# First slot's steps and the fixed rows' read three half steps sooner, clearing writes with the first steps, weights' loads one place sooner

## The chip, the cores and the metric

One NeuronCore of a Trainium2 chip runs the whole kernel as one launch. The metric is the device time of that launch in microseconds (us), lower is better. Engines are called PE (TensorE, matmuls), PEld (its weight loads), DVE (VectorE), ACT (ScalarE), POOL (GpSimd) and SP (SyncE, which here issues most of the transfers). XS, SD and ZD are scratch buffers in device memory.

## The reference, cut to what matters

```python
# x: 8 x 2496 x 256, filt: 1249 x 256, 8 experts, w1: 8 x 256 x 1024, w2: 8 x 1024 x 256
X = np.fft.rfft(x, axis=1)
y = np.fft.irfft(X * (filt_r + 1j * filt_i), n=2496, axis=1)   # a long filter along the sequence
x = y.reshape(19968, 256)
xn, en = x / norm(x), expert_emb / norm(expert_emb)
logits = xn @ en.T / tau
expert_idx = argmax(logits)                      # one expert a row
gate_w = softmax(logits)[expert_idx]
for e in range(8):
    mask = expert_idx == e
    h = np.maximum(x[mask] @ w1[e], 0.0)
    out[mask] = gate_w[mask, None] * (h @ w2[e])
```

## The kernel before

**Groups and stages.** The eight batches are eight groups, 0 to 7. The transform of length 2496 is taken as 64 times 39, and every group goes through three stages. `conv_s1` (11 tiles): a tile of x is read (`in`), multiplied by a matrix of cosines (`s1_g_t` in PSUM), copied by ACT to `s` and written to the buffer SD. `conv_s2` (10 tiles): `a` is read from SD, the other half of the transform is taken (`s2_g_k`), the product with the filter `f` (read from in_filt) is formed as `yy` and `xs`, transformed back (`sa`), copied to `z` and written to ZD. `conv_sb`: `f` is read from ZD, the last matmul gives `y`, the rows of the result; these become `rows` (16-bit high and low pieces), are transposed (`tp`, `yT`) for the logits `lp`, and `route` finds each row's expert: `l`, `mx`, `oh`, `ex` on DVE and ACT, the ranks `rk` on PE, then the target addresses `ixi`. POOL scatters `rows` by these into XS, which is sorted by expert.

**Slots.** Rows sorted in XS are worked off in slots. The rows of the first six tiles of group 0 (chunk 0, twelve scatters) go to slots 0 to 7, one an expert, of 128 rows: the "fixed" slots, in areas of XS that are set to zero ahead by `clear_fixed(e)`, one write `XS<-zf` an expert. `read_pair(p)` reads the areas of two experts, each with a transposing read (`xTf`) and one of two columns (`metaf`). Later slots have 256 rows. A slot has four half steps: each does `up` (matmuls `ph`, 12 for a fixed slot, and their halves `h` by ACT and DVE) and, two steps later, `down` (matmuls `po`). The output rows are scattered by POOL.

**Weights.** Expert e's two matrices come as loads of 1024 KB (`W<-in_w`, the last expert's in pieces of 256 KB). They are prepared in steps, named by a letter, the expert and a piece in the tables below: g is a sum of squares on PE (`gram`), d, p and q make a scale of it, k makes a high 16-bit piece on ACT (`W<-W,wsc`, L324), l the low one on DVE (L331). A slot's `ph` and `po` read these pieces.

**Order.** All engines but POOL have an order written out by hand over the head of the kernel, a loop in which step n takes one step of the convolution, then what the tables give it, then a half step of a slot:

```python
for n in range(HEAD):
    next(whole_head, None)
    weights(n)          # clear_fixed at CLEAR..CLEAR+7, read_pair(0) at FIRST_ROWS, WLOADS, WPREP
    keep_warm(n)
    if n >= SLOTS:
        next(steps)
```

Steps 0 to 10 are group 0's `conv_s1`, 11 to 34 its `conv_s2`, from 35 on its `conv_sb`, with group 1's `conv_s1` between from 43. The convolution has 79 steps, so that steps 79 to 81 hold the tables' work and slots alone. After the head, half steps of slots and the convolutions of groups 1 to 7 are emitted in turn by a pace, the steps in `WLATE` with them (by the count of half steps done; slot e's first is number 4e), and a scheduler sets the order of the engines. A transfer issued by SP or ACT takes one of eight completion counters in turn; the issue waits until the transfer that had the counter eight places ahead has landed. POOL's transfers have eight of their own.

Of the kernel before, what the change touches and what calls it, by code (L numbers as in the profile page):

```python
# [46 lines left out]
DLAG = 2  # L47
MID = 8
XNEXT = 43
WLOADS = (38, 40, 42, 44, 46, 48, 50, 52, 54, 56, 58, 60, 61, 63, 78, 79)  # L50
WPREP = {43: "g00", 44: "g01", 46: "d0", 48: "p0", 49: "q0 g10", 50: "k00", 51: "l00 k01 g11", 52: "d1 l01 k02",
# [5 lines left out]
WLATE = {16: "l52 k53 p6", 17: "l53 q6 g70", 18: "k60 g71", 19: "d7 l60 k61", 20: "l61 k62", 21: "l62 k63 p7",  # L57
         22: "l63 q7", 23: "k70", 24: "l70 k71", 25: "l71 k72", 26: "l72 k73", 27: "l73"}
SIDE = 18
CLEAR, FIRST_ROWS = 39, 64  # L60
SLOTS, HEAD = 66, 82
WARM = {-1: 8, 12: 26, 35: 22, 40: 6}
FRONT = 0
FIXED = 128
# [10 lines left out]
def moe_spectral_kernel(  # L75
# [810 lines left out]
    def read_pair(p):  # L886

        xT = mp2.tile([P, 4, 256], F16, tag="xT", name=f"xTf{p}")
        for j in range(2):
            e = 2 * p + j  # L890
            meta = mpm.tile([P, 2, 2], F32, tag="meta", name=f"metaf{e}")[:, :1]
            pairs[e] = xT[:, :, j * FIXED:(j + 1) * FIXED], meta
            at = slice(e * CAP, e * CAP + FIXED)
            read_rows(0, *pairs[e], XS16[at, 0:2 * D], XS[at, D:D + 2], fixed=True)
        last.setdefault("read", last["sp"])
# [151 lines left out]
    def weights(n):  # L1047
# [3 lines left out]
        if n == FIRST_ROWS:  # L1051
            read_pair(0)
        if n in WLOADS:
            next(loads)
# [62 lines left out]

    begun, late = [], dict(WLATE)

# [132 lines left out]
```

## Time and profile before

| | |
|---|---|
| time, median of 3 runs | 1350.24 us (1348.65 to 1364.11) |
| profiled execution | 1344.95 us |
| its span | 1343.2 us |
| PE busy | 1246.3 us, 93% of the span |
| DVE, ACT, POOL busy | 938.8 (70%), 762.2 (57%), 489.2 us (36%) |
| chain of work that ended last | PE 71%, DMA 18%, DVE 4%, issue 3%, ACT 2% |
| mean granted clock of PE | 0.97 |

The profiled execution is one run beside the three. PE is the busiest engine, and most of the chain that ended last lies on it. The share of the span says little of a stretch: the kernel's first 300 us are bound now by transfers, now by short steps on several engines.

### The profile page before, as it was taken

To read this page: it belongs to the slowest core of one execution; us is meant where nothing else is said; L and a number is where in the kernel's file an instruction comes from. 1 tells how busy PE (TensorE), PEld (TensorE's weight loads), DVE (VectorE), ACT (ScalarE), POOL (GpSimd) and SP (SyncE) were. 2 spreads that over 40 slices of the span, in tenths; PEclk is the share of its full clock that TensorE was granted. 3 is DMA by queue.
4 is the path that set the end of the run, shared out by engine and by line. 5 is a ranking of instruction groups with operands and counts; after the bars stand their busy time and mean duration, and the time that the engine had idled before them with its cause. 6 is when DMAs were issued, how large, how long until landed. Compare 5 with 4: busy or idle time off the path is not lost.

```text
span 1343.2 us, 36499 instructions
## 1 busy us (share of the span) xinstructions
PE 1246.3 (93%) x11027; PEld 981.2 (73%) x11027; DVE 938.8 (70%) x3078; ACT 762.2 (57%) x1760; POOL 489.2 (36%) x569
## 2 busy tenths in 40 slices
PE   7867899959897999998999999999999999999997
PEld 2344686627584778786888788878887888889886
DVE  1455796756586688976889697868786885444664
ACT  2175466825664586667757785678465843233333
POOL 0003322264255325541464346423633175111221
PEclk9997899979998999998999999999999999999999
DMA  7899868887868697868769887777675544221221
GB/s 230 271 325 369 246 185 217 186 229 226 200 169 238 190 202 174 226 192 184 168 182 245 193 195 203 224 186 194 173 196 140 119 119 106 54 49 41 57 45 37
DMA packets 272354, 241.27 MB, mean 180 GB/s; under 512 B 167123, under 2 KB 212182, under 8 KB 270373
## 3 DMA queue, kind: packets, MB, share of 16 engines
q1 hardware_dynamic: 243965, 177.87, 52.0%
q0 software_dynamic: 24320, 57.97, 14.8%
q10 hardware_dynamic: 3880, 3.03, 0.7%
q8 instruction: 104, 1.70, 0.6%
q14 instruction: 85, 0.70, 0.2%
HBM read 122.32 MB, written 85.57 MB: 155 GB/s over the span
## 4 chain that ended last, share of the span: by engine, by line
PE 71%; DMA 18%; DVE 4%; issue 3%; ACT 2%; POOL 1%; SPq 1%; ACTq 0%; DVEq 0%; POOLq 0%
PE ph L967 27%; PE po L992 26%; PE s L444 5%; DMA yT<-rows 4%; DMA f<-ZD 3%; PE sa L444 3%; PE y L444 2%; DMA f<-in_filt 2%; DMA W<-in_w 2%; PE s L439 2%; PE sa L555 2%; DMA XS<-rows,ixi 1%; DMA SD<-s 1%; PE y L439 1%; PE lp L610 1%
## 5 line engine op out<-in xcount | busy, mean ns | idle before, releaser
L992 PE MATMUL po<-W,h 128*128 (+1 forms) x3824 | 494.4, 273 | 0.2 <-ACT h L975 0.2
L967 PE MATMUL ph<-xT,wp 128*128 128x256 f16 (+2 forms) x4224 | 471.6, 258 | 10.9 <-DMA xT<-XS 3.7
L967 PEld LDWEIGHTS <-wp 128*128 128x128 f16 x4224 | 357.7, 98 | 87.8 <-issue 41.6
L992 PEld LDWEIGHTS <-h 128*128 128x128 f16 x3824 | 361.2, 98 | 68.9 <-issue 26.4
L975 ACT ACTIVATE h<-ph 128x512 f16<-128x512 f32 (+2 forms) x384 | 201.7, 527 | 244.9 <-PE ph L967 182.2
L1007 POOL DMA_INDIRECT out_dram<-o,meta x153 | 158.5, 1036 | 305.9 <-ACT o L1006 228.6
L976 DVE SCALAR_TENSOR_TENSOR h<-ph,h 128x512 f16<-128x512 f32 (+2 forms) x384 | 227.1, 591 | 48.3 <-ACT h L975 46.6
L951 DVE COPY wp<-W 128x1024 f16 x352 | 164.8, 469 | 117.8 <-PE ph L967 115.3
L790 POOL DMA_INDIRECT XS<-rows,ixi x176 | 180.1, 1023 | 142.0 <-issue 93.8
L536 POOL TENSOR_TENSOR yy<-yy,xs 128x512 f32<-128x512 f32 x60 | 80.5, 1343 | 105.6 <-DVE xs L499 85.0
L497 DVE TENSOR_TENSOR yy<-s,f 128x256 f32<-128x256 f32 x160 | 61.3, 417 | 62.5 <-ACT xs L529 27.8
L400 POOL DMA_DIRECT2D in<-in_x x66 | 38.8, 588 | 168.8 <-DVE xp L413 57.3
L635 DVE SCALAR_TENSOR_TENSOR rows<-y,rr,rows 128x256 f16<-128x256 f32 x176 | 76.7, 477 | 23.8 <-ACT rows L632 23.1
L668 ACT ACTIVATE rows<-y 128x256 f16<-128x256 f32 x176 | 67.3, 398 | 26.5 <-PE y L439 24.3
L1006 ACT ACTIVATE o<-po,meta 128x256 f32<-128x256 f32 x148 | 64.0, 478 | 28.8 <-PE po L992 27.3
L632 ACT ACTIVATE rows<-y,rr 128x256 f16<-128x256 f32 x176 | 75.5, 496 | 7.5 <-DVE rr L673 5.8
L558 ACT COPY z<-sa 128x512 f32<-128x512 f32 x80 | 46.7, 584 | 49.9 <-PE sa L555 41.2
L465 ACT COPY s<-s 128x512 f32<-128x512 f32 x88 | 52.7, 600 | 27.8 <-PE s L439 15.9
L595 ACT COPY yT<-tp 128x512 f16<-128x512 f16 x99 | 58.6, 605 | 9.1 <-PE tp L593 5.4
L444 PE MATMUL s<-xp,c1h 117*128 117x512 f32 (+1 forms) x144 | 62.0, 438 | 0.0
L412 ACT CAST yp<-yy 128x512 fp32r<-128x512 f32 x50 | 30.9, 619 | 53.0 <-POOL yy L536 52.5
L610 PEld LDWEIGHTS <-yT 128*128 128x128 f16 x704 | 33.2, 98 | 35.5 <-DMA yT<-rows 17.9
(208 smaller groups left out, 1688.8 us busy)
## 6 DMA issues: line engine op xcount, KB each, us to landing
f<-in_filt SPq DMA_DIRECT2D x160, 256.0 KB
a<-SD SPq DMA_DIRECT2D x80, 256.0 KB
ZD<-z SPq DMA_DIRECT2D x80, 256.0 KB
f<-ZD SPq DMA_DIRECT2D x80, 240.0 KB
SD<-s SPq DMA_DIRECT2D x70, 240.0 KB
in<-in_x POOLq DMA_DIRECT2D x66, 234.0 KB
W<-in_w SPq DMA_DIRECT2D x14, 1024.0 KB
in<-in_x SPq DMA_DIRECT2D x22, 234.0 KB
```

Of the source, the lines that this page charges most:

```text
L444: nc.tensor.matmul(out_, w[:k], b, start=(n == 0), stop=(n == 2))
L536: nc.gpsimd.tensor_tensor(out=yy, in0=yy, in1=xs, op=ALU.add)
L632: nc.scalar.activation(rows[:, i, 0:D], y[:, i], AF.Copy, scale=rr[:, u:u + 1])
L635: nc.vector.scalar_tensor_tensor(out=rows[:, i, D:2 * D], in0=y[:, i], scalar=rr[:, u:u + 1], in1=rows[:, i, 0:D], op0=ALU.mult, op1=ALU.s ...
L668: nc.scalar.activation(rows[:, i, D:2 * D], y[:, i], AF.Square, accum_out=ssq[:, u + i:u + i + 1])
L790: i = nc.gpsimd.indirect_dma_start(out=XS, out_offset=bass.IndirectOffsetOnAxis(ap=ix, axis=0), in_=src, in_offset=None)
L951: last["dve"] = nc.vector.tensor_copy(wp, src)
L967: last["pe"] = nc.tensor.matmul(ph[:, fi, :size], wp[:, k * 2 + wh, fi * P:(fi + 1) * P], xT[:, xh * 2 + k, :size], start=(c == 0), stop=( ...
L975: last["act"] = nc.scalar.activation(h[:, 0, :, :size], ph[:, :, :size], AF.Relu)
L976: last["lo"] = nc.vector.scalar_tensor_tensor(out=h[:, 1, :, :size], in0=ph[:, :, :size], scalar=0.0, in1=h[:, 0, :, :size], op0=ALU.max, ...
L992: nc.tensor.matmul(self.po[:, s], h, self.Wp[:, off + wh * 1024:off + wh * 1024 + D], start=(fp == 0 and fi == 0 and c == 0), stop=(fp == ...
L1007: i = nc.gpsimd.indirect_dma_start(out=out, out_offset=bass.IndirectOffsetOnAxis(ap=self.meta[:n, s, 0:1].bitcast(I32), axis=0), in_=o, in ...
```

## The change

Only the tables and constants of the head change. The eight clearing writes go from steps 39 to 46 to steps 1 to 8. Each load of weights takes the place in which the one before it stood; the first goes from step 38 to 32. `read_pair(0)`, at step 64 before, stands at 61; the first half step of a slot at 63, not 66; the head ends with its last step of convolution. The preparation of weights up to piece l20 stays at its steps; from there on the steps move sooner by one or two in n, while they come later as counted by half steps of slots: expert 5's l50 and l51, at steps 80 and 81 (14 and 15 half steps done), come at 16 and 17.

```diff
-WLOADS = (38, 40, 42, 44, 46, 48, 50, 52, 54, 56, 58, 60, 61, 63, 78, 79)
+WLOADS = (32, 38, 40, 42, 44, 46, 48, 50, 52, 54, 56, 58, 60, 62, 75, 76)
...
-         75: "d5 l40 k41", 76: "l41 k42", 77: "l42 k43 p5", 78: "l43 q5 g60", 79: "k50 g61", 80: "d6 l50 k51",
-         81: "l51 k52"}
-WLATE = {16: "l52 k53 p6", 17: "l53 q6 g70", 18: "k60 g71", 19: "d7 l60 k61", 20: "l61 k62", 21: "l62 k63 p7",
-         22: "l63 q7", 23: "k70", 24: "l70 k71", 25: "l71 k72", 26: "l72 k73", 27: "l73"}
...
+         74: "d5 l40 k41", 75: "l41 k42", 76: "l42 k43 p5", 77: "l43 q5 g60", 78: "k50 g61"}
+WLATE = {16: "d6 l50 k51", 17: "l51 k52", 18: "l52 k53 p6", 19: "l53 q6 g70", 20: "k60 g71", 21: "d7 l60 k61",
+         22: "l61 k62", 23: "l62 k63 p7", 24: "l63 q7 k70", 25: "l70 k71", 26: "l71 k72", 27: "l72 k73", 28: "l73"}
 SIDE = 18
-CLEAR, FIRST_ROWS = 39, 64
-SLOTS, HEAD = 66, 82
+CLEAR, FIRST_ROWS = 1, 61
+SLOTS, HEAD = 63, 79
```

Lines of the changed kernel have numbers lower by one. On SP in the first stage (in0_t is tile t of x, SD0 the buffer written for group 0, zf the zeros), before:

```order
L400 DMA in0_4_258<-in_x 117x512
L467 DMA SD0_208<-s0_1_262 120x2x256
L400 DMA in0_5_265<-in_x 117x512
L467 DMA SD0_208<-s0_2_269 120x2x256
L400 DMA in0_6_272<-in_x 117x512
L467 DMA SD0_208<-s0_3_276 120x2x256
```

and now:

```order
L399 DMA in0_4_258<-in_x 117x512
L466 DMA SD0_208<-s0_1_262 120x2x256
L346 DMA XS_224<-zf_225 128x258
L399 DMA in0_5_266<-in_x 117x512
L466 DMA SD0_208<-s0_2_270 120x2x256
L346 DMA XS_224<-zf_225 128x258
L399 DMA in0_6_274<-in_x 117x512
L466 DMA SD0_208<-s0_3_278 120x2x256
```

A clear stands behind each of SD0_1 to SD0_8; they stood among the reads of f from ZD before, at f0_4 to f0_8. W0, the first load of weights, stands ahead of the write of ZD0_9, the last tile of `conv_s2(0)`; ahead of f0_7's read four loads stand behind ZD0_9 in both, ahead of f0_10's seven.

On SP at the fixed rows' read (which waits for the twelfth scatter of chunk 0 in both; in1_10 is group 1's last tile of x), before:

```order
L400 DMA in1_10_1286<-in_x 117x512
L264 DMA W_201<-in_w1 128x2048
L264 DMA W_201<-in_w2 128x2048
L878 DMA_TRANSPOSE xTf0_1393<-XS_224 128x4x128
L879 DMA metaf0_1394<-XS_224 128x2
L878 DMA_TRANSPOSE xTf0_1393<-XS_224 128x4x128
L879 DMA metaf1_1397<-XS_224 128x2
L878 DMA_TRANSPOSE xTf1_1477<-XS_224 128x4x128
L879 DMA metaf2_1478<-XS_224 128x2
```

and now:

```order
L263 DMA W_201<-in_w1 128x2048
L399 DMA in1_10_1287<-in_x 117x512
L877 DMA_TRANSPOSE xTf0_1308<-XS_224 128x4x128
L878 DMA metaf0_1309<-XS_224 128x2
L877 DMA_TRANSPOSE xTf0_1308<-XS_224 128x4x128
L878 DMA metaf1_1312<-XS_224 128x2
L263 DMA W_201<-in_w2 128x2048
L877 DMA_TRANSPOSE xTf1_1429<-XS_224 128x4x128
L878 DMA metaf2_1430<-XS_224 128x2
```

The two loads that stood ahead of pair 0, W12 and W13, now stand ahead of in1_10 and between pair 0 and pair 1.

On ACT at the end of the head (s1_9 and s1_10 are the last tiles of group 1's first stage, ex and ixi belong to the routing of tile 6, h0_0_0 is the first half of slot 0), before:

```order
L467 DMA SD1_209<-s1_9_1364 120x2x256
L465 COPY s1_10_1378<-s1_1_10_1375 128x512
L467 DMA SD1_209<-s1_10_1378 120x256
L467 DMA SD1_209<-s1_10_1378 40x256
L745 ACTIVATE ex0_6_1387<-l0_6_1367 128x80
L770 CAST ixi0_6_1432<-ix0_6_1430 128x10
L324 ACTIVATE W_201<-W_201,wsc_205 128x1024
L975 ACTIVATE h0_0_0_1455<-ph0_0_0_1442 128x2x128
```

and now:

```order
L466 DMA SD1_209<-s1_9_1372 120x2x256
L974 ACTIVATE h0_0_0_1395<-ph0_0_0_1382 128x2x128
L464 COPY s1_10_1401<-s1_1_10_1398 128x512
L466 DMA SD1_209<-s1_10_1401 120x256
L466 DMA SD1_209<-s1_10_1401 40x256
L323 ACTIVATE W_201<-W_201,wsc_205 128x1024
L974 ACTIVATE h0_0_1_1440<-ph0_0_1_1420 128x2x128
L744 ACTIVATE ex0_6_1410<-l0_6_1375 128x80
```

h0_0_0 stands ahead of the copy and the writes of s1_10, and a piece of W and h0_0_1 ahead of ex0_6. SD1_10's two writes take the counters of xTf1's second read and of metaf3, where they took those of its first and of metaf2. On PE, ph0_0_0 (12 matmuls) stands ahead of s1_1_10 and ph0_0_1 ahead of rk0_6; both stood behind rk0_6. From group 1's `conv_s2` (s2_1_0) to its first routing (rk1_0) PE has 452 matmuls ph, 222 po and 112 gram, where it had 492, 243 and 96; the other matmuls there are the same. From group 2's `conv_s2` (s2_2_0 and ph2_0_0) to the end the order is the same on every engine.

## Rows read from the trace of the kernel before

**Rows 1.** Busy time by stage: stretch, its length, engines' busy time (instructions), PEclk, DMA, GB/s

```profile
10.00:25.00 15.00, 11.43 (x28) 3.81 (x27) 3.26 (x20) 5.61 (x11) 0.00 (x0) 0.89 0.86 272
...
59.00:67.00 8.00, 6.59 (x27) 2.83 (x26) 0.22 (x1) 0.59 (x1) 0.00 (x0) 1.00 0.47 135
67.00:104.00 37.00, 26.21 (x237) 15.66 (x236) 20.63 (x70) 26.59 (x73) 2.21 (x2) 0.95 1.04 326
104.00:126.00 22.00, 15.48 (x81) 7.97 (x80) 11.04 (x51) 13.29 (x29) 13.08 (x14) 0.70 1.01 363
126.00:142.00 16.00, 8.76 (x72) 5.84 (x71) 8.93 (x25) 5.87 (x9) 0.00 (x0) 0.82 1.06 320
142.00:260.00 118.00, 113.32 (x1112) 85.39 (x1111) 95.26 (x305) 75.52 (x172) 30.31 (x42) 0.97 0.77 208
260.00:299.00 39.00, 23.92 (x177) 14.09 (x175) 24.12 (x138) 17.07 (x42) 27.45 (x28) 0.78 0.82 226
299.00:1343.00 1044.00, 1002.56 (x9212) 830.70 (x9211) 757.83 (x2421) 609.63 (x1411) 414.61 (x466) 0.99 0.64 159
```

**Rows 2.** The chain of waits, 0 to 170 us: start, length, what

```profile
19.45 3.11 DMA in<-in_x
...
90.56 13.14 DMA f<-ZD
...
125.71 10.87 DMA SD<-s
```

**Rows 3.** Timeline of PE, 60 to 165 us: start, length, instruction, [idle before <- releaser]

```profile
90.63 1.10 PE L439 MATMUL y<-f,csb_sb 120*128 120x512 f32 x2 [3.02 <-DMA f<-ZD]
...
95.85 2.04 PE L439 MATMUL y<-f,csb_sb 120*128 120x512 f32 x2 [1.56 <-DMA f<-ZD]
...
141.03 0.23 PE L753 MATMUL rk<-oh,lt 128*128 128x80 f16 x1 [5.43 <-DVE oh L743]
...
148.66 1.93 PE L439 MATMUL s<-a,c_sb 128*128 128x512 f32 x4
```

**Rows 4.** The chain of waits, 255 to 305 us

```profile
279.94 5.10 DMA XS<-rows,ixi
...
290.24 5.52 DMA XS<-rows,ixi
...
295.77 3.44 DMA xT<-XS
```

**Rows 5.** Timeline of POOL, 225 to 300 us

```profile
260.52 1.04 POOL L790 DMA_INDIRECT XS<-rows,ixi  x1 [5.07 <-issue]
```

**Rows 6.** DMA issues of the whole kernel: count, KB each

```profile
W<-in_w SPq DMA_DIRECT2D x14, 1024.0 KB
...
XS<-zf SPq DMA_DIRECT2D x8, 129.0 KB
```

**Rows 7.** Timeline of POOL, 60 to 165 us

```profile
123.15 0.98 POOL L790 DMA_INDIRECT XS<-rows,ixi  x1 [0.30 <-issue]
```

**Rows 8.** Timeline of SP, 56 to 160 us

```profile
125.44 0.89 SPq L264 DMA_DIRECT2D W<-in_w  x2
130.53 1.34 SPq L878 DMA_TRANSPOSE xTf<-XS  x1
...
138.98 0.58 SPq L879 DMA_DIRECT2D metaf<-XS  x1
...
144.28 6.66 SPq L479 DMA_DIRECT2D a<-SD  x6
```

**Rows 9.** Timeline of ACT, 60 to 165 us

```profile
104.16 0.28 ACT L745 ACTIVATE ex<-l 128x96 f32<-128x96 f32 x1 [1.10 <-DMA f<-ZD]
...
139.65 0.73 ACTq L467 DMA_DIRECT2D SD<-s  x2
```

**Rows 10.** The chain of waits, 158 to 170 us

```profile
161.29 0.67 PE ph L967 x12
161.96 0.66 PE po L992 x6
162.62 0.92 PE gram L286 x16
```

**Rows 11.** Timeline of DVE, 60 to 165 us

```profile
145.67 1.28 DVE L331 SCALAR_TENSOR_TENSOR W<-W,wsc 128x1024 f16<-128x1024 f32 x1
```

4 rows, old and new, of the table WPREP are left out of this document.

## The prediction

> **What bounds the kernel now.** I read the busy time by stage first [rows 1]. From 299 µs to the end PE is busy 1002.56 of 1044 µs, and the order of all engines there is the same in both kernels; the reader is to see that nothing of this change can act behind 299 µs but a common shift. All of it is decided in the 299 µs ahead. There the stages have different limits. In the first (10 to 25 µs) the core's DMA engines are taken 0.86 of the time at 272 GB/s and PE waits for transfers; the chain of waits [rows 2] shows an x tile's read on it (19.45, 3.11 µs). From 67 to 104 the DMA share is 1.04 at 326 GB/s, and the chain runs through a 13.14 µs read of f from ZD: this stage is bound by transfers, 14 loads of 1024 KB of weights among them [rows 6]. From 104 to 142 it is a chain of short steps on all engines, with PE at 15.48 of 22 and 8.76 of 16 µs. From 142 to 260 PE is busy 113.32 of 118, so there PE's queue, that is the work ordered ahead, sets the time. From 260 to 299 PE has 23.92 of 39: it waits for group 1's rows. The chain [rows 4] shows it: scatter after scatter on POOL to 290.24, 5.52 for the last to land, 3.44 for xT, then ph2_0_0 at 299.26. The first of them starts at 260.52 [rows 5]; 22 scatters and two output writes follow each other without a hole, so what moves the first scatter moves all that follows by as much. I work out by how much.
>
> **The change, part by part.**
> Clears in the first stage. Eight writes of 129 KB [rows 6], 1.06 MB, go onto SP's queue behind SD0_1 to SD0_8. At the stage's 272 GB/s they take 3.9 µs. Of its 15 µs, 0.14 is not taken, 2.1 µs [rows 1]. So the cost is 3.9 − 2.1 = 1.8 if every gap is filled, 3.9 if none is. I take +2.5, nearer to the first, since SP issues the clears behind the loads of the next tile and the reads run ahead. SP's own time for them is covered, as it waits for the step's copy anyway.
>
> Weights one place sooner. W0 now stands ahead of ZD0_9's write and of the first reads of ZD. 1.05 MB is 3.2 µs at 326 GB/s, and from 59 to 67 the DMA share is 0.47, which leaves 4.2 of 8 µs free. It hides unless it sits in front of that write: 0 to +1, I take +0.5. Each later load takes the place of the one before it; ahead of f0_7 there are still four behind ZD0_9, ahead of f0_10 seven, so I cost the rest at nothing; what hides it is that the stage's bytes stay the same.
>
> Clears gone from 67 to 104. 1.06 MB less at 326 GB/s is 3.2 µs. The stage's last consumer shows that bytes decide: y0_7 and y0_8 waited 3.02 and 1.56 for f from ZD [rows 3], and the landing of that read released ex0_0 at 104.16 [rows 9]. So −3.2, with 0 at the other end, if the weights fill the room; bytes that are no longer there can't cost.
>
> The fixed rows' read. It waits for the last of chunk 0's twelve scatters. That scatter started at 123.15 [rows 7]; SP sent two W loads at 125.44 (over at 126.33) and then stood until 130.53 [rows 8]: 7.4 µs from scatter to read. At the end of group 1 the same kind took 5.10 and 5.52 [rows 4]. Now one of the two W loads stands ahead of in1_10 and the other behind pair 0. I take the nearest row, 5.10: −2.3. Ends: 0, and −4.2, where the read goes out as soon as SP was free (126.33).
>
> The end of the head. Pair 1 stands behind W13, and SD1_10's two writes, issued on ACT, take completion counters that pair 1's transfers hold. Before, they went out at 139.65, right behind the last of pair 1's commands at 138.98 [rows 8, 9]. If W13 goes wholly ahead of pair 1 the wait is its 3.2 µs. Queued behind it on ACT are a piece of W, h0_0_1 and ex0_6, and a1_0's read waits for these writes. Pair 1's read would otherwise go out 2.3 sooner, which covers most of it: 0 to +3.2, I take +0.5.
>
> Slot steps sooner. ph0_0_0 now stands ahead of rk0_6, and PE idled 5.43 µs ahead of rk0_6 [rows 3], so it is covered as far as the read comes in time. That is work which PE no longer has between group 1's second stage, which begins at 148.66 there [rows 3], and that group's first routing: by the two orders 40 matmuls ph and 21 po fewer, 16 gram more. In the dense part 12 ph take 0.67, 6 po 0.66 and 16 gram 0.92 [rows 10]: 40 × 0.056 = 2.2, 21 × 0.11 = 2.3, less 0.9, that is −3.6. As PE is busy 96% of 142 to 260, it should reach the first scatter in full; the other end is 0.
>
> Sum: 2.5 + 0.5 − 3.2 − 2.3 + 0.5 − 3.6 = −5.6. It is made against the profiled execution (1344.95, its span 1343.2): 1339.35. That execution lies 5.3 under the median of the runs shown, so the forecast is 1350.24 − 5.6 = **1344.6**. With every term at its best: 1.8 + 0 − 3.2 − 4.2 + 0 − 3.6 = −9.2, 1341.0; at its worst: 3.9 + 1 + 0 + 0 + 3.2 + 0 = +8.1, 1358.3.
>
> **The rivals.**
> A. The read is not sooner, though it stands sooner. The 7.4 µs are then not the two W loads': whether those stand in SP's queue or are sent a little sooner, their bytes share the engines with the scatter. For it: the share from 104 to 142 is full (1.01 and 1.06). Against it: a write issued by ACT at 125.71, thus on another queue, took 10.87 µs beside the two loads [rows 2]; loads do delay what other queues send. Term of the read at 0: −3.3, 1346.9. (The Trainium skill, "DMA: Bandwidth & Descriptors", "Queues, rings and completion order", says that each DMA engine takes the rows of queues in turn, a packet of each; by that rule a scatter on POOL's row would not stand behind all of a W load on SP's, and the read would be as late as before, 1346.9. The 10.87 µs of ACT's write speak against it in part.)
>
> B. The order's gain is not in the end. The first scatter is released by DVE's routing or by ACT, and not by PE's place; its row names no releaser [rows 5]. DVE is busy 95.26 of 118 there [rows 1]. Then the work that PE does sooner leaves a hole further on. Term at 0: −2.0, 1348.2.
>
> C. Slower: the preparation of weights comes too late for the slots. Slot e of the fixed rows needs expert e's pieces, and the change leaves fewer slot steps between the last pieces of an expert and its slot: expert 5's l50 and l51 stood 6 and 5 half steps ahead of slot 5, now 4 and 3; those of 7 one less than before. A low piece is 1.28 µs on DVE [rows 11], and DVE is full to 81%. If slots 5, 6 and 7 each wait for two pieces, 3 × 2 × 1.28 = 7.7: +2.1, 1352.3. It decides from the point at which more than 5.6 / 1.28 = 4.4 pieces are on PE's path; below that the kernel is still faster. Against it: a half step with its gram matmuls is 0.67 + 0.66 + 0.92 = 2.25 µs of PE by [rows 10], so three of them are 6.7 µs, room for five low pieces, and an expert's own pieces are needed one after the other.
>
> D. All terms at their best: 1341.0. The stage from 67 to 104 would have to give all of the clears' time, the first stage to hide what it can, and the read to go out when SP is free.
>
> **How the numbers follow.** The forecast (−5.6) gets 0.40, A 0.17, B 0.18, C 0.13, D 0.12. They lie between 1341.0 and 1352.3. The profiled execution and the median differ by 5.3, and I add half of that on both sides for the median that the runs of the changed kernel may have: 1338 to 1355. What is left out is mostly the worst end, 1358.3. A measurement of this kernel tells a change of about 2% from none, 27 µs here; no case and neither end reaches 1323 or 1377, so within 2% gets 0.95, and 0.02 and 0.03 go to what I have not seen.
>
> **What would show it.** In the profile after: the first stage some 2 µs longer, with reads of x longer; no wait of 3 µs for f from ZD ahead of y0_7; the first xTf read at about 128 and not 130.53; ph0_0_0 at about 134, ahead of the last s1_1 tiles; a1_0's read at 142 to 143 (144.28 before); group 1's first scatter at about 255 (260.52) and ph2_0_0 near 293.7 (299.26), with the same length from there on. The read at 130 or more speaks for A; a hole of PE between 200 and 260 with the scatter at 258 for B; PE waiting for a W piece or a wp copy in slots 5 to 7 for C. I would be wrong altogether if the first stage lost more than 8.1 µs, which is all that the other terms give together at the values taken, or if a completion counter held SP or ACT at another place than those named.

## The result

The changed kernel takes 1363.36 us (median of 20 runs, 1357.62 to 1374.22), the kernel before 1350.48 (20 runs beside them): ratio 1.0095, 95% interval 1.0078 to 1.0112. That is 12.9 us slower, where 5.6 faster was forecast, and outside the range of 1338 to 1355. The profiled execution took 1366.8 us, its span 1365.0. Runs e6 to e15 were taken where the kernel before itself takes 1472 us (mean granted clock 0.93 there, 0.97 in its other runs); every ratio below is against the kernel before in the same set of runs.

The stages of the changed kernel, in the view of [rows 1]:

```profile
10.00:25.00 15.00, 10.08 (x19) 2.81 (x17) 3.26 (x20) 4.47 (x9) 0.00 (x0) 0.77 0.91 279
...
59.00:67.00 8.00, 6.87 (x23) 2.82 (x23) 2.37 (x6) 1.32 (x3) 0.00 (x0) 1.00 0.84 288
67.00:104.00 37.00, 25.67 (x203) 14.50 (x202) 17.63 (x64) 24.86 (x71) 2.21 (x2) 0.89 0.98 310
...
142.00:260.00 118.00, 102.94 (x973) 75.75 (x973) 89.54 (x259) 67.63 (x145) 28.57 (x40) 0.94 0.77 209
260.00:299.00 39.00, 29.36 (x306) 21.79 (x305) 28.11 (x176) 21.00 (x62) 19.48 (x22) 0.85 0.75 178
```

The same slices of time now hold less of the program: from 10 to 25 us PE ran 19 instructions and not 28, from 142 to 260 it ran 973 and not 1112. The lost time builds up along the program. At these marks the changed kernel is later than the kernel before by (us, one execution each): first read of a from SD 3.6, first read of f from ZD 4.6, first scatter of chunk 0 5.9, the fixed rows' read 6.9, a1_0's read 9.2, group 1's first scatter 10.4, its last 15.25, ph2_0_0 15.5. The two longest steps are the first stage and the end of group 1.

The first stage on PE, changed kernel, and its last line in the kernel before:

```profile
16.08 1.10 PE L438 MATMUL s<-in,c_sb 117*128 117x512 f32 x2 [2.06 <-DMA in<-in_x]
...
18.35 7.09 PE L438 MATMUL s<-in,c_sb 117*128 117x512 f32 x8 [0.99 <-DMA in<-in_x]
```

```profile
18.41 3.88 PE L439 MATMUL s<-in,c_sb 117*128 117x512 f32 x6
```

A matmul takes 0.89 us in the one row and 0.65 in the other. The granted clock of this stage was 0.77, and 0.89 before: behind its waits for x, PE had the lower of its two levels (1.2 GHz, not 2.4) for 6.8 us here, for 3.4 before.

SP of the changed kernel, by its timeline. The first line answers to 26.73 in the kernel before, the next three to the start of `conv_sb`, the others to [rows 8]:

```profile
30.32 1.27 SPq L478 DMA_DIRECT2D a<-SD  x3
...
62.12 0.43 SPq L263 DMA_DIRECT2D W<-in_w  x1
64.84 0.32 SPq L558 DMA_DIRECT2D ZD<-z  x1
68.19 1.81 SPq L392 DMA_DIRECT2D f<-ZD  x4
...
127.88 0.38 SPq L263 DMA_DIRECT2D W<-in_w  x1
...
137.41 1.31 SPq L877 DMA_TRANSPOSE xTf<-XS  x1
...
141.41 0.44 SPq L263 DMA_DIRECT2D W<-in_w  x1
...
143.13 0.58 SPq L878 DMA_DIRECT2D metaf<-XS  x1
...
153.47 4.98 SPq L478 DMA_DIRECT2D a<-SD  x6
```

PE and ACT at the same places, by their timelines:

```profile
92.59 1.10 PE L438 MATMUL y<-f,csb_sb 120*128 120x512 f32 x2
98.54 0.21 PE L609 MATMUL lp<-ent,yT 128*128 128x16 f16 x2 [3.48 <-ACT yT L594]
...
140.53 0.83 PE L966 MATMUL ph<-xTf,W 128*128 128x128 f16 x12 [1.63 <-DMA xTf<-XS]
...
150.30 0.22 PE L752 MATMUL rk<-oh,lt 128*128 128x80 f16 x1 [7.05 <-DVE oh L742]
```

```profile
94.31 1.15 ACT L320 ACTIVATE W<-W,wsc 128x1024 f32<-128x1024 f32 x1 [2.04 <-DVE wsc L303]
...
147.54 0.32 ACTq L466 DMA_DIRECT2D SD<-s  x1
147.91 0.38 ACT L974 ACTIVATE h<-ph 128x256 f16<-128x256 f32 x1 [5.67 <-DMA metaf<-XS]
...
150.94 0.26 ACT L744 ACTIVATE ex<-l 128x80 f32<-128x80 f32 x1
```

Two of my signs came true and helped nothing. The wait of 3.02 for f ahead of y0_7 [rows 3] is gone, but PE waits 3.48 for yT right behind it, since ACT stands in a piece of W whose scale DVE has only just made (94.31). And ph0_0_0 is ahead of the last tiles of s1_1, but rk0_6, which waited 5.43, now waits 7.05: SD1_9's write (147.54) needs the counter of metaf2, whose transfer took 4.33 us behind W13, and ACT with h0_0_0 and ex0_6 stands behind that write.

Between a1_0's read and group 1's first scatter PE stands idle for 8.7 us, where it was 4.7. Most of it are two waits, for f from ZD and for yT; the last line is the wait for f in the kernel before:

```profile
234.51 1.13 PE L438 MATMUL y<-f,csb_sb 120*128 120x512 f32 x2 [3.85 <-DMA f<-ZD]
...
257.23 0.22 PE L609 MATMUL lp<-ent,yT 128*128 128x16 f16 x2 [2.97 <-DMA yT<-rows]
```

```profile
225.89 1.12 PE L439 MATMUL y<-f,csb_sb 120*128 120x512 f32 x2 [1.41 <-DMA f<-ZD]
```

The end of group 1 on POOL, which answers to [rows 4, 5], and on PE (rk1_0 is at 266.93, rk1_4 at 284.66):

```profile
270.95 0.99 POOL L789 DMA_INDIRECT XS<-rows,ixi  x1 [0.60 <-issue]
...
280.35 0.97 POOL L789 DMA_INDIRECT XS<-rows,ixi  x1 [0.30 <-DVE wp L950]
...
281.74 1.02 POOL L1006 DMA_INDIRECT out_dram<-o,meta  x1 [0.16 <-ACT yT L594]
287.29 0.98 POOL L789 DMA_INDIRECT XS<-rows,ixi  x1 [4.54 <-DVE ixi L781]
...
297.55 1.01 POOL L1006 DMA_INDIRECT out_dram<-o,meta  x1 [0.30 <-DMA XS<-rows,ixi]
...
305.49 0.89 POOL L789 DMA_INDIRECT XS<-rows,ixi  x1 [0.30 <-issue]
```

```profile
266.93 0.19 PE L752 MATMUL rk<-oh,lt 128*128 128x64 f16 x1
...
269.82 0.21 PE L609 MATMUL lp<-ent,yT 128*128 128x16 f16 x2 [0.83 <-DMA yT<-rows]
...
282.35 0.21 PE L609 MATMUL lp<-ent,yT 128*128 128x16 f16 x2 [1.69 <-DMA yT<-rows]
...
284.66 0.19 PE L752 MATMUL rk<-oh,lt 128*128 128x64 f16 x1
```

The same two marks, and POOL's ninth scatter, in the kernel before:

```profile
257.17 0.19 PE L753 MATMUL rk<-oh,lt 128*128 128x64 f16 x1
...
270.73 0.19 PE L753 MATMUL rk<-oh,lt 128*128 128x64 f16 x1
```

```profile
273.50 0.99 POOL L790 DMA_INDIRECT XS<-rows,ixi  x1 [0.30 <-issue]
```

In the kernel before, eight scatters, two output writes, eight and six scatters followed each other without a hole, 29.7 us from first to last. Now there is a hole of 4.54 behind the first eight, and o1_3's output write stands between the second eight and the last six: 34.5 us. The hole ends with ixi of the second chunk, which comes from rk1_4 (284.66). From rk1_0 to rk1_4 it is 17.7 us; it was 13.6. The two orders tell why: 48 matmuls ph and 39 po stood between the two before, 76 and 38 now. Those 28 ph are 1.6 us of PE, and the two waits for yT, which weren't there, 2.5. Before, PE stood idle for 0.02 us there, so there was no room for more work.

From ph2_0_0 to the end the order is the same, and the 9212 matmuls shown there are the same (kernel before, then the changed kernel):

```profile
299.26:1343.20 1043.94, 1002.56 (x9212) 830.70 (x9211) 757.57 (x2420) 609.63 (x1411) 414.61 (x466) 0.99 0.64 159
```

```profile
314.80:1365.00 1050.20, 1006.76 (x9212) 831.27 (x9211) 757.67 (x2423) 609.04 (x1411) 415.43 (x466) 0.99 0.63 158
```

The 6.3 us between them are hardly the change's: e4, with the changed kernel's order there, takes 1040.8. So the pair of traces overstates the loss, and the median of 20 runs, +12.9, is its size.

### The profile page after: what moved, and what is told of

Its sections match the earlier page's. It is cut to its first block, busy times and chain, and to the rows that moved or that the text cites. A ratio compares the mean times of both kernels' runs of the same rounds, so it can differ in the third digit from the quotient of the medians.

```text
span 1365.0 us, 36498 instructions
## 1 busy us (share of the span) xinstructions
PE 1258.1 (92%) x11027; PEld 982.6 (72%) x11027; DVE 940.1 (69%) x3078; ACT 761.7 (56%) x1760; POOL 489.5 (36%) x569
## 4 chain that ended last, share of the span: by engine, by line
PE 65%; DMA 13%; DVE 4%; issue 4%; ACT 3%; POOL 2%; SPq 1%; DVEq 0%; POOLq 0%; ACTq 0%
PE ph L966 25%; PE po L991 24%; PE s L443 4%; DMA yT<-rows 4%; PE sa L443 2%; PE y L443 2%; DMA f<-ZD 2%; PE s L438 2%; PE sa L554 2%; PE y L438 1%; DMA a<-SD 1%; DMA XS<-rows,ixi 1%; DMA xT<-XS 1%; PE lp L609 1%; PE tp L592 1%
## 5 line engine op out<-in xcount | busy, mean ns | idle before, releaser
L991 PEld LDWEIGHTS <-h 128*128 128x128 f16 x3824 | 361.4, 98 | 73.4 <-issue 29.9
L464 ACT COPY s<-s 128x512 f32<-128x512 f32 x88 | 52.5, 598 | 35.6 <-PE s L438 21.2
```

The source lines that it names most:

```text
L991: nc.tensor.matmul(self.po[:, s], h, self.Wp[:, off + wh * 1024:off + wh * 1024 + D], start=(fp == 0 and fi == 0 and c == 0), stop=(fp == ...
```

## The experiments

In each the edit is against the kernel before unless said otherwise. The letters of theories and rivals in the expectations are their own, not those of the prediction.

**e1 to e4: the parts of the change alone.** The clears alone:

```diff
-CLEAR, FIRST_ROWS = 39, 64
+CLEAR, FIRST_ROWS = 1, 64
```

> The kernel before with the eight clears alone moved to steps 1 to 8. Theory A (the losses add up part by part): the clears' bytes hold up the first stage, so that the first read a of SD goes out at about 30.3 us as in the changed kernel (26.73 before), and nothing is given back behind 67 us, because the chain there runs over DVE and ACT (the scale of expert 0 and its first piece) and not over the reads of f: +3.6 us, 1.0027. Rival B (the stage from 67 to 104 is bound by bytes, as I had forecast): first stage +3.6, then -3.2: +0.4, 1.0003. Rival C (the clears are nearly all of the loss, by what they do to all later transfers): +10 or more, 1.0075.

Measured: 1.0035 (1.0005 to 1.0065), 4.7 us. In its trace a's first read is at 32.32:

```profile
32.32 1.27 SPq L479 DMA_DIRECT2D a<-SD  x3
```

The loads alone (last two at 78, 79 as before):

```diff
-WLOADS = (38, 40, 42, 44, 46, 48, 50, 52, 54, 56, 58, 60, 61, 63, 78, 79)
+WLOADS = (32, 38, 40, 42, 44, 46, 48, 50, 52, 54, 56, 58, 60, 62, 78, 79)
```

> The kernel before with the loads of weights alone one place sooner (the two of the last expert stay). Theory A: W0 in front of ZD0_9's write delays the first read of f by 1.0 us (68.19 - 63.55 less the 3.59 that were lost already) and nothing else changes, as the fixed rows' read has no 1024 KB load other than those already there: +1.0, 1.0008. Rival B (hidden, since the stage had free transfer time): 0, 1.000. Rival C (loads sooner are the gain I forecast at the read): -2, 0.9985, with the first xTf read at about 128.

Measured: 1.006 (1.0034 to 1.0085). That is more than the 1 us that its trace loses from a's first read to f's; see e6.

Read, slots and the weights' steps alone: FIRST_ROWS 61, SLOTS 63, HEAD 79, both tables of the change, the last two loads at 75 and 76.

> The kernel before with the fixed rows' read and the slots' steps three half steps sooner, the weights' preparation with them, clears at their old place and loads at theirs (the two loads that stood ahead of pair 0 now stand between pair 0 and pair 1). Theory A: this part makes most of the loss, 12.9 - 4.6 = 8 us: the loads between the pairs delay metaf2, whose counter SD1_9's write needs, and with it ex0_6 and a1_0 on ACT and SP; with two loads there instead of one it is not less than that: +8, 1.006, a1_0's read 5 us or more later than 144.28. Rival B (as forecast): -5.4, 0.996, a1_0 sooner than 144.

Measured: 1.0065 (1.0042 to 1.0089), 8.8 us. The size is theory A's, the place is not: a1_0's read is 1.6 us late, group 1's first scatter even 0.5 sooner than in the kernel before, and ph2_0_0 7.7 late. Most of it is lost between the first eight scatters and the rest:

```profile
269.25 0.97 POOL L789 DMA_INDIRECT XS<-rows,ixi  x1 [0.30 <-DVE wp L950]
270.64 1.02 POOL L1006 DMA_INDIRECT out_dram<-o,meta  x1 [0.17 <-ACT yT L594]
278.64 0.98 POOL L789 DMA_INDIRECT XS<-rows,ixi  x1 [6.98 <-DVE ixi L781]
```

So theory A fell in its main part, and theory D was formed: the loss is the order of the end of group 1.

The changed kernel with CLEAR = 39:

> The changed kernel with the clears alone put back to steps 39 to 46. Theory A: 12.9 - 3.6 = +9.3 us against the kernel before, 1.007, first stage as before (a0_0's read at 26.7), SD1_9's write still behind W13. Rival B (what the clears take is given back later): +12.5, 1.0093. Rival C (the clears are nearly all of the loss): +1 or less, 1.0005.

Measured: 1.0069 (1.0039 to 1.0099), 9.3 us: by the medians the clears are 3.6 of the 12.9.

**e9 and e10: which edit reorders the end of group 1.** Both tables of the weights' steps as in the change, all else as before:

> The kernel before with the two tables of the weights' preparation alone as in the changed kernel (steps sooner in the head, but later as counted by half steps of slots); read, slots, loads and clears at their old places. Theory D (the slots' part loses its time at the end of group 1: with the late preparation the scheduler puts 76 and not 48 matmuls ph between rk1_0 and rk1_4, and o1_3's output write behind the second eight scatters, so POOL stands idle ahead of those): +7 us, 1.005, with a hole of 4 us or more on POOL behind the first eight scatters and rk1_4 17 us or more behind rk1_0 (13.56 in the kernel before). Rival E (the loss comes from the head, where loads stand between the pairs of reads and SD1_9's write waits): 0, 1.000, as the head's order on SP is the old one.

Measured: 1.005 (1.0021 to 1.0078), the loss without any slot step sooner. Its order differs in group 3 too (that of e10 as well), so it doesn't stand alone.

Read, slots, the last two loads and the weights' steps from step 66 on all three steps sooner, the late table as before:

```diff
-CLEAR, FIRST_ROWS = 39, 64
-SLOTS, HEAD = 66, 82
+CLEAR, FIRST_ROWS = 39, 61
+SLOTS, HEAD = 63, 79
...
-         61: "l13 q2 g30", 62: "k20 g31", 63: "l20", 64: "d3", 66: "k21 p3", 67: "l21 k22 q3", 68: "l22 k23 g40",
+         61: "l13 q2 g30", 62: "k20 g31 l20 d3", 63: "k21 p3", 64: "l21 k22 q3", 65: "l22 k23 g40",
```

> The kernel before with read and slots three half steps sooner, and the weights' preparation moved three steps sooner with them, so that it stands at the same half step of a slot as before; loads and clears at their old places, so that W12 and W13 stand between pair 0 and pair 1. The order from rk1_0 to group 2 is that of the kernel before. Theory D: without the reordered end of group 1 what is left is the head's own effect, by the profile of the slots' part alone -0.5 at group 1's first scatter: -3 to +2 us, 0.998 to 1.0015, no hole on POOL. Rival E: +8, 1.006, as with the slots' part of the change.

Measured: 1.0018 (0.9989 to 1.0047). This speaks against rival E, but with another order in group 3 it doesn't settle it; e12 and e13 do. In this set of runs POOL has a hole there in every kernel, with the order before too (11 to 14 us from the eighth to the ninth scatter), which I had not expected. PE stands idle between rk1_0 and rk1_4 for 5.1 to 6.7 us in all ten traces of this set, much of it with nothing that the profile shows as its cause; with the order of before it was 0.0 to 0.2 in the first set. So these runs test what the reorder costs, and not how the 13.6 us became 17.7.

**e6: the first load alone** at step 32, the others at their places:

> The kernel before with the first load of weights alone at step 32, ahead of ZD0_9's write; the other loads at their old places. Theory: its bytes delay the write and so the first read of f by 1.0 us, and all behind: +1, 1.0008. Rival F (all of what the loads' part costs, 8 us by its runs and 4.3 at ph2_0_0 by its profile, comes by this one load): +4 or more, 1.003. Rival G (W0 is at hand sooner, and the chain over expert 0's scale ends sooner): -1 or less.

Measured: 1.0061 (1.003 to 1.0092). It looks like rival F, but the order of this kernel, and that of e2, differs from the kernel before in group 3 as well (PE's matmuls 2667 to 3750, counted in order of time), which the change's order doesn't. So these two say nothing of the change's loads, and whether W0 or group 3 makes their 0.6% is not shown. The pair with one order to the end, e4 against e3, gives 1.0069 and 1.0065. That agrees with a cost of the size of the 0.9 us in the traces, and with intervals of 0.3% it can't tell it from nothing.

**e11 to e13: the reorder by itself, and undone.** One step of the tables:

```diff
-         22: "l63 q7", 23: "k70", 24: "l70 k71", 25: "l71 k72", 26: "l72 k73", 27: "l73"}
+         22: "l63 q7", 23: "k70", 24: "l70 k71", 25: "l71 k72", 26: "l72 k73", 28: "l73"}
```

> The kernel before with one step moved: l73, the last low piece of the last expert, at half step 28 and not 27, as in the changed kernel. Head and stages up to group 1's slots are those of the kernel before; the scheduler's order from rk1_0 to rk1_8 is that of the changed kernel, word for word on PE (76 matmuls ph between rk1_0 and rk1_4, o1_3's output write behind the second eight scatters), and from ph2_0_0 on it is the same in all. Theory D (the reordered end of group 1 makes most of the loss): +6 to +8 us, 1.005, nothing lost ahead of 220 us. Rival E (the head makes it): 0, 1.000. Rival K (only e9's other differences, in group 3, made e9 slower): 0 as well.

Measured: 1.0039 (1.0005 to 1.0073). POOL of this run, and of e7 (the order before), of the same set:

```profile
278.62 0.97 POOL L784 DMA_INDIRECT XS<-rows,ixi  x1 [0.31 <-issue]
287.86 1.01 POOL L1001 DMA_INDIRECT out_dram<-o,meta  x1 [8.02 <-ACT o L1000]
292.48 0.98 POOL L784 DMA_INDIRECT XS<-rows,ixi  x1 [3.61 <-DVE ixi L776]
...
302.75 1.01 POOL L1001 DMA_INDIRECT out_dram<-o,meta  x1 [0.31 <-issue]
```

```profile
274.41 0.97 POOL L790 DMA_INDIRECT XS<-rows,ixi  x1 [0.30 <-issue]
277.93 1.01 POOL L1007 DMA_INDIRECT out_dram<-o,meta  x1 [2.38 <-ACT o L1006]
285.07 1.06 POOL L1007 DMA_INDIRECT out_dram<-o,meta  x1 [6.13 <-DVE l L764]
286.67 0.99 POOL L790 DMA_INDIRECT XS<-rows,ixi  x1 [0.54 <-issue]
```

From the eighth to the ninth scatter it is 13.86 against 12.26, and o1_3's write at 302.75 takes one place more. From group 1's first scatter to ph2_0_0 the traces of this set keep apart by their order: 52.5 and 52.6 us with the change's (e9, e11), 47.4 to 48.9 in the eight with that of before. One late step of 1.28 us on DVE, moved by one half step of a slot, changed PE's order over a stretch of some 570 matmuls. PE of e7 in that place, with waits of the kind named above:

```profile
273.89 0.20 PE L610 MATMUL lp<-enz,yT 128*128 128x16 f16 x2 [1.12 <-issue]
```

The slots' part, e3, with the order of before kept (edit against e3):

```diff
-         74: "d5 l40 k41", 75: "l41 k42", 76: "l42 k43 p5", 77: "l43 q5 g60", 78: "k50 g61"}
-WLATE = {16: "d6 l50 k51", 17: "l51 k52", 18: "l52 k53 p6", 19: "l53 q6 g70", 20: "k60 g71", 21: "d7 l60 k61",
-         22: "l61 k62", 23: "l62 k63 p7", 24: "l63 q7 k70", 25: "l70 k71", 26: "l71 k72", 27: "l72 k73", 28: "l73"}
+         74: "d5 l40 k41", 75: "l41 k42", 76: "l42 k43 p5", 77: "l43 q5 g60", 78: "k50 g61 d6 l50 k51"}
+WLATE = {16: "l51 k52 l52 k53 p6", 17: "l53 q6 g70", 18: "k60 g71", 19: "d7 l60 k61", 20: "l61 k62", 21: "l62 k63 p7",
+         22: "l63 q7", 23: "k70", 24: "l70 k71", 25: "l71 k72", 26: "l72 k73", 27: "l73"}
```

> The kernel before with read and slots three half steps sooner as in the change and its table of the head's weights' steps, but d6, l50 and k51 in the head's last step and the late table as before, so that the scheduler's order from rk1_0 to the end is that of the kernel before; clears and loads at their old places. Theory D: -2 to +2 us, 0.9985 to 1.0015. Rival E: +6 or more, 1.0045, as the head's order on SP, ACT and PE is that of the change.

Measured: 1.0016 (0.9977 to 1.0056). The same edit in the whole change:

> The changed kernel with its weights' steps put as in the run before: the clears in the first steps, the loads one place sooner, read and slots three half steps sooner, but the order from rk1_0 on that of the kernel before. Theory D with A: what is left are the clears (+3.6) and W0 (+1.0): +4 to +6 us against the kernel before, 1.0035, and 7 less than the changed kernel. Rival E: +12, 1.009, as the changed kernel.

Measured: 1.0018 (0.9982 to 1.0054), where the change itself has 1.0095. With clears, loads, read and slots all where the change puts them, and only these late steps back, most of the loss is gone; the two intervals don't meet.

**e7, e8, e14, e15: what a clear costs.** Small clears at the old place:

```diff
-        nc.sync.dma_start(XS[e * CAP:e * CAP + FIXED], zr.bitcast(I32))
+        nc.sync.dma_start(XS[e * CAP:e * CAP + FIXED, D:D + 2], zr.bitcast(I32)[:, D:D + 2])
```

> The kernel before with its clears at their old place (steps 39 to 46), each writing the two columns of addresses and gates alone; left out is the writing of zeros into the data columns, 1.06 MB between 67 and 104 us. Order of all engines as before. Theory A (nothing is given back there, since the chain from y0_0 to the first scatter runs over DVE and ACT): 0, 1.000, first scatter within 1 us of the kernel before. Rival B (bytes bound this stage, as I forecast): -3.2, 0.9976, first scatter 3 us sooner behind the first read of f.

Measured: 0.9967 (0.9937 to 0.9998), faster than both kernels, if narrowly. But its first scatter is 45.9 us behind the first read of f, not sooner than in the others. The same with CLEAR = 1:

> The kernel before with the clears at steps 1 to 8, each writing the two columns of addresses and gates alone (1 KB for 129 KB); left out is the writing of zeros into the data columns. Theory (bytes): the transfers of x are not held up, the first read a of SD at 27.2 or sooner: 0 to +0.5 us, 1.000. Rival H (eight more commands on SP and eight places of completion counters hold up the stage): first read a at 29 or later, +3, 1.002. If the bytes that are gone from 67 to 104 do count: -3, 0.998.

Measured: 1.0001 (0.9967 to 1.0036), a's first read at 28.87. That lies between the traces without clears (26.35 to 27.71) and those with whole ones (29.89 to 32.32), though almost no bytes are written; so rival H, the commands and counters, is not excluded for a part. Two sets of whole clears at the old place (e14) and, with CLEAR = 1, in the first steps (e15):

```diff
         nc.sync.dma_start(XS[e * CAP:e * CAP + FIXED], zr.bitcast(I32))
+        nc.sync.dma_start(XS[e * CAP + FIXED:e * CAP + 2 * FIXED], zr.bitcast(I32))
```

> The kernel before with twice the clears at their old place: each step writes a second 128 rows of the same expert's area with the same zeros (1.06 MB more between 67 and 104 us). Order of all engines but SP as before. If bytes there cost what taking them away gained: +4.8 us, 1.0033. If the chain there runs over the engines and hides them (theory A): 0, 1.000.

Measured: 1.0076 (1.0048 to 1.0105), 11 us for 1.06 MB more. In its trace 52.75 us lie between the first read of f and the first scatter (45.4 in the mean with one set), and PE waits there:

```profile
78.73 1.09 PE L286 MATMUL gram<-W 128*128 128x128 bf16 x16 [2.22 <-DMA W<-in_w]
...
95.96 2.05 PE L440 MATMUL y<-f,csb_sb 120*128 120x512 f32 x2 [4.14 <-DMA f<-ZD]
...
103.56 1.21 PE L440 MATMUL y<-f,csb_sb 120*128 120x512 f32 x2 [2.80 <-DMA f<-ZD]
```

> The kernel before with the clears at steps 1 to 8, each with a second write of the same size (2.11 MB in the first stage, none behind). If the first stage pays for every byte: twice the 3.6 us of one set, a's first read at 34 us or later, +7 us less what is given back from 67 on (0 to 4.8): +2.5 to +7, 1.002 to 1.005, and well above what one set costs there. If the later stages take it up: 0 to +2, 1.001.

Measured: 1.0032 (1.0003 to 1.0062), a's first read at 34.12. The first stage pays for the second set too. How much is open: against the mean without clears it is 7.1 us, twice the 3.8 of one set, but against e1, where PE's clock was as low (0.74 up to that read, 0.75 here), 1.8. What the later stage gets back is lost in an interval of 0.4 to 9 us.

## Why the prediction was wrong

With 16 traces the head's terms can be measured as means over kernels with an edit and without it, which takes out much of what one execution has by chance. The last two rows use the first set of runs alone.

| step of the sum | forecast | measured | from |
|---|---|---|---|
| clears in the first stage | +2.5 | +3.8 | a's first read: 27.06 without (11 traces), 30.84 with one set (3) |
| W0 ahead of ZD0_9 | +0.5 | +0.9 | from there to the first read of f: 37.02 without (11), 37.91 with (5) |
| clears gone from 67 to 104 | -3.2 | -0.4 | first read of f to first scatter: 45.37 with (9), 45.02 without or small (6) |
| fixed rows' read | -2.3 | -0.7 | twelfth scatter to read: 7.66 in the old order (10), 6.98 in the new (6) |
| end of the head | +0.5 | +0.9 | read to a1_0's read: 16.35 (10), 17.27 (6) |
| order, to group 1's first scatter | -3.6 | +0.4 | a1_0 to that: 115.08 (before, e1, e2), 115.44 (e3, e4, changed) |
| order, first scatter to ph2_0_0 | 0 | +6.7 | 38.91 (before, e1, e2), 45.61 (e3, e4, changed) |

The measured column adds up to +11.6, near the +12.9 of the runs. Single traces spread widely, so only two rows stand clear of chance: the first (26.4 to 27.7 without, 29.9 to 32.3 with) and the last (38.4 to 39.6 before, 43.9 to 47.0 changed). In the other five the ranges overlap, and they can't be told from nothing.

**The step that failed** is the one on which the sum was hung: "what moves the first scatter moves all that follows by as much". It took the row of POOL, dense in the kernel before, for a law. The last scatter is released by the routing of the second and third chunk, and their place in PE's order changed too. The row was dense by a hair: the ninth scatter starts 2.77 us behind rk1_4 in the kernel before, without waiting for it, and 2.63 in the changed one, where it does wait for ixi. I counted 40 matmuls ph fewer ahead of rk1_0 and took them for work that PE no longer had. But from rk1_8 on the order is the same. Only 12 of the 40 had gone ahead of s2_1_0; the other 28 come back between rk1_0 and rk1_4, and of the po 16 come back between rk1_4 and rk1_8. From s2_1_0 to rk1_8 PE has 12 ph and 6 po fewer and 16 gram more, which is 0.4 us less at the prediction's own prices (0.67 + 0.66 - 0.92). So that term could give next to nothing, and the longer end of group 1 costs 6.7.

Nor did the term of -3.6 reach the first scatter, which is 0.4 later behind a1_0. PE was busy for 2.5 us less up to there (means of the same three traces each), but stood idle for 2.9 more, mostly for f from ZD (3.2 to 3.85, against 1.3 to 1.5) and, less evenly, for yT. With less work ahead of it PE came sooner to what transfers had not yet brought. I also had o1_3's write on POOL moved behind the second eight scatters in the order, and priced it at nothing; it is 1.3 us on that path (297.55 to the next scatter). That the reorder costs this time is shown by e11, which has it alone, by e13, which has all but it, and by the traces, which part by their order in both sets; e3 against e12 agrees, though their intervals meet. Its size is less sure: 6.7 us in the traces of the first set, 4.4 in those of the second, 6 in the runs of e11 (1 to 11), 10 between the change and e13. That one late step of the tables makes the scheduler do it is shown by e11.

**Clears.** That the first stage pays was right, and the term too small, 3.8 for 2.5. I let the reads "run ahead", and they did not: PE waited 2.06 for a tile of x at 16.08, where it had waited 0.53. And the sum had no term for the clock. Up to a's first read the mean granted clock was 0.89 in the changed kernel. Three traces without clears had 0.88 (e2, e10, e12); they have that read at 27.6 to 27.7, and against those the changed kernel's 30.32 is 2.7 later, near my 2.5. With e1 the clock was 0.74 and the read at 32.32. So part of the 3.8 seems to be a lower clock behind the waits, though e13 (0.83, the read at 29.89) fits this less well. How much of the rest is bytes and how much commands stays open (e8). The give-back of 3.2 was wrong in the trace: once the wait for f is gone, the wait for yT takes its place. The prediction's 14 loads "among them" were too many as well: ten of the fourteen go out by 104 us, in both kernels. Yet the runs say that bytes there have a price (e7 0.9967, e14 1.0076). In e14 the waits for f and W show where; for what e7 gains, no place was found, and its interval nearly touches 1. By the medians the net of moving one set lies between 0 (e13 against e12, with the loads) and 4.7 us (e1); the changed kernel against e4 gives 3.6.

**The read and the end of the head.** Rival A was right: the read is hardly sooner, 0.7 of 2.3, and in the first set of runs not at all (7.8 in the new order, 7.4 in the old, three traces each). A load sent elsewhere on SP's queue still shares the engines with the scatter, which took 8.82 us from its start to its landing here with only one 1024 KB load sent right ahead of it (127.88). The Trainium skill, "DMA: Bandwidth & Descriptors", "Queues, rings and completion order", has each DMA engine take the rows of queues in turn. The small difference of the two means agrees with it, and the spread (5.52 to 8.84) forbids more. The wait that W13 makes between the pairs was in the sum and is there: metaf2 took 4.33 us, and ex0_6, a1_0 and rk0_6 waited for it. It came one place ahead of what I had named, though, which I had called a sign of being wrong: SD1_9's write needed metaf2's counter, and not SD1_10's two. On average it costs 0.9, since a1_0's read is late in the other kernels too.

**The rivals.** B was right in what came of it, the order's term at nothing, and the hole of PE in its sign is there, at 234.51 and 257.23. But the first scatter still follows rk1_0, by 4.02 us (3.35 before); what held PE up ahead of rk1_0 were transfers, and not DVE's or ACT's routing. D fell with the terms that it took at their best. C named the late preparation as the danger, with the wrong mechanism: PE waits for no piece of W in slots 5 to 7 of the changed kernel; the late steps cost time by what they did to the scheduler's order. None of the cases had the end of group 1 longer than before.

## What to carry to other kernels

When an edit takes work off a queue ahead of one mark, find where it went: if the order further on is the same, it stands either sooner or between the mark and there, and what it lands in front of is what to price. Compare the order at every release on the path, the last as well as the first, and every engine that carries the path. In a program whose order a scheduler sets, one small step can reorder a distant stage, so a part of a change tried alone has to be compared in its order before its time is read.

## What was not expected of the hardware

Bytes in the full stage from 67 to 104 us may not be priced evenly: 1.06 MB taken away gave 0.33%, as much added cost 0.76%, but the intervals (0.02 to 0.63, 0.48 to 1.05) meet. A few waits for x in the first stage are followed by up to 17 us at PE's lower clock (e1), which lengthens the stage beyond the waits. And executions of one order differ: from ph2_0_0 to the end, with the same 9212 matmuls, 1040.8 (e4), 1043.9 (before) and 1050.2 us (changed), 0.9% of a part where the order is the same.
